# Register-addressed hardware loops for the products with wq and w3, and 15 small loads at the end, in a decode kernel on one core

## The chip, the cores and the metric

The kernel runs on one core of a Trainium2 chip. The metric is the device time of one execution in microseconds (us), the median of several runs. One execution was also taken by the hardware profiler; its instructions and transfers are what is called the trace here. The engines are TensorE (PE, whose weight loads have a row of their own, PEld), VectorE (DVE), ScalarE (ACT), GpSimd (POOL) and SyncE (SP). A name with a q behind it (PEldq, DVEq, SPq) stands for instructions that the engine's sequencer works off by itself: register arithmetic, branches, waits, and the issue of DMAs.

## What is computed

Two branches on the same two rows of x, mixed by a gate (`Sk` is 16384, `D` 1024, 32 heads of 128, `F` 3584; all inputs bf16):

```
g = sigmoid((x * gate_w).sum(-1))
q = x @ wq                                  # 1024 x 4096, in 32 heads
a = softmax(q k_cache^T * 128**-0.5) v_cache, heads joined, @ wo
h = gelu(layernorm(x) @ w1), shifted along the sequence
x1 = x + h @ w2                             # with one token the shift leaves zeros
b = x1 + gelu(layernorm(x1) @ w3) @ w4      # w3: 1024 x 3584, w4: 3584 x 1024
out = g * a + (1 - g) * b
```

There are 64 pairs of batch row and head. K and V of one pair are 4 MB (2^22 bytes) each, so the two caches make up 537 of the 570 million bytes that one execution reads.

## The kernel before

**The plan.** The program is written as a list of operations for each engine (`_Plan`). `pl.add` appends an instruction with the events that it waits for, and gives it an event of its own if it is to signal; an event is a semaphore and a count. `emit` writes the lists out. For TensorE, DVE and ACT the 32 rounds over the caches are written as a hardware loop of 16 turns with two rounds each (L100); inside it each wait compares with a count held in a register (L72), and one DVE instruction (L703) writes to an address held in a register. All that stands ahead of the rounds is written out in full, instruction by instruction.

**The ring.** All weights and caches pass through a ring in SBUF of five slots of 32 KB in each partition (4 MB a slot). SP issues every load of it, in one fixed order: wq (slots 0, 1), w2 (slot 2), w3 (3, 4), w4 (0, 1), then K and V of round 0, K and V of round 1 and so on, and the two halves of wo last, the second in six pieces. K of a round takes slots 2 and 3 or 3 and 4 by turns, V takes 0 and 1. A load is issued when the readers of its slots have released them (`release`, `pump`). So w4 waits for the last product with wq, K of round 0 waits for the reader of slot 3, and V of round 0 waits for the last product with w4.

**The prologue on TensorE.** x is transposed (L589). The product with wq (L604) has 8 steps over the rows of wq and 32 heads in each, 256 products of a 128x128 weight block with two columns, all into one PSUM bank; the first one of all clears the bank (`start`). DVE copies q out (L609). The products with w2 (L510) and the layer norm of x1 (L401 to L444) follow. The product with w3 (`dense_stage`, L468 to L490, matmul at L477) is put on the list eight times, once for each of the eight groups of rows of w3, with 28 output blocks each, 224 products. Slot 3 holds the first 16384 of a partition's 28672 elements, so it is released after the fifth group and slot 4 after the eighth. GELU (L454 to L462) and the product with w4 (L510) end the prologue; the row b goes to PSUM (L526, L529).

**The rounds.** DVE transposes K in place (L647), TensorE makes the scores (L653), DVE, ACT and TensorE the softmax, TensorE the product with V (L689), and L703 stores the pair's row.

**The end.** The heads are joined, the product with wo (L728) is added to the row in PSUM, DVE copies out each half (L757), and SP and ACT store a quarter each of either half (L760). All engines then meet (L789), SP waits for the last two stores, and its increment of a semaphore (L792) ends the program.

Of the kernel before, what the change touches and what calls it, by code (L numbers as in the profile page):

```python
# [9 lines left out]
BF16 = mybir.dt.bfloat16  # L10
# [13 lines left out]
class _Plan:  # L24
# [18 lines left out]
    def add(self, eng, fn, waits=(), sig=False, dyn=False):  # L43

        ev = None
        if sig:
            self.cnt[eng] += 1
            ev = _Ev(self.esem[eng], self.cnt[eng])
        self.ops[eng].append((self._merge(waits), fn, ev, 1, dyn))
        return ev  # L50

    def dma(self, eng, fn, sem, waits=()):
        key = sem.num
# [55 lines left out]
def _cdiv(a, b):  # L109
    return (a + b - 1) // b  # L110
# [10 lines left out]
def build_kernel(nc, A_x, A_k, A_v, A_wq, A_wo, B_w1, B_w2, B_w3, B_w4, gate_w, out, dbg=None):  # L121
    dbg = dbg or {}
    B, Sq, D = A_x.shape
    _, H, Sk, Dh = A_k.shape
    F = B_w3.shape[1]
# [13 lines left out]
    NBD = D // P  # L139
    NBF = F // P  # L140
    NRS = 5
    SLOT = J * Dh
# [25 lines left out]
    with ExitStack() as st:  # L168
        inner = st.enter_context(ExitStack())
        block = inner.enter_context(nc.Block())  # L170
        sb = lambda name, shape, dt: st.enter_context(nc.sbuf_tensor(name, shape, dt))
# [14 lines left out]
        xT_bf = sb("xT_bf", [P, NBD, 2], BF16)  # L186
# [30 lines left out]
        xn_bf = sb("xn_bf", [P, NBD, 2], BF16)  # L217
# [9 lines left out]
        banks = [st.enter_context(nc.psum_tensor(f"ps{i}", [P, 512], F32)) for i in range(8)]  # L227
        sem = lambda n: st.enter_context(nc.semaphore(n))
# [8 lines left out]
        pl = _Plan(esems)  # L237
# [38 lines left out]
        for hp in range(HP):  # L276
# [7 lines left out]
                    waits=(ev_rowm,), sig=True)  # L284
# [4 lines left out]
                        waits=(e0,), sig=True)  # L289
# [16 lines left out]
        def pump():  # L306
            while dma_q and all(i in slot_free for i in dma_q[0][2]):
                key, fns, slots = dma_q.pop(0)
                waits = sum((slot_free.pop(i) for i in slots), ())
                slot_of[key] = slots[0]  # L310
                slots_of[key] = slots
                for k, fn in enumerate(fns):
                    dsem = s_ring[slots[0]] if len(fns) == 1 else s_tail[k]
                    dma_done[key] = dma_done[key, k] = pl.dma("sp", (lambda e, fn=fn, idx=slots[0]: fn(e, idx)), dsem,
                                                              waits=waits if k == 0 else ())

        def release(key, ev, slots=None):
            for idx in slots or slots_of[key]:
                assert idx not in slot_free
                slot_free[idx] = tuple(ev) if isinstance(ev, (tuple, list)) else (ev,)  # L320
            pump()

        def arrived(key):
            assert key in dma_done, f"load {key} not yet issued in program order (would deadlock)"
            return dma_done[key]
# [50 lines left out]
        hs_ps, h3_ps = r3(hs_ps2d), r3(h3_ps2d)  # L376
        bc_nb = lambda ap2: ap2.unsqueeze(1).broadcast_to([P, NBD, 2])
        b5_rd = []
        evd = {}
# [3 lines left out]
        def pe_b5(fn, waits=(), sig=False):  # L383
            ev = pl.add("pe", fn, waits=tuple(waits) + tuple(b5_rd) + (evd["b5zero"],), sig=sig)
            del b5_rd[:]
            if sig:
                b5_lw[0] = ev
            return ev

        def b5_wrote(ev):  # L390
            b5_lw[0] = ev
# [73 lines left out]
        def cols(wv, kl, nb, nout):  # L465
            return wv[:, kl, :].rearrange("p (q r) -> p r q", r=nout)[:, nb, :]

        def dense_stage(key, kls, nkw, nout, out_ps, rhs_of, rhs_key, done_key, width):  # L468
            def run():
                wv = ring_w(slot_of[key], nkw, width)  # L470
                ev_arr = arrived(key)
                ev = None
                first = True
                for nb in range(nout):
                    for kl in kls:
                        lastmm = (nb == nout - 1 and kl == kls[-1])
                        fn = lambda e, nb=nb, kl=kl: e.matmul(  # L477
                            out_ps[:, nb, :], lhsT=cols(wv, kl, nb, nout), rhs=rhs_of(kl),
                            start=False, stop=True, skip_group_check=True)
                        if first:  # L480
                            ev = pe_b5(fn, waits=(ev_arr, evd[rhs_key]), sig=lastmm)
                            first = False
                        else:
                            ev = pl.add("pe", fn, sig=lastmm)
                for j, slot in enumerate(slots_of[key]):
                    if kls[-1] == _cdiv(min(nkw * width, SLOT * (j + 1)), width) - 1:
                        release(key, ev, (slot,))
                b5_wrote(ev)
                evd[done_key] = ev
            return run  # L490

        def st_x1():
# [44 lines left out]
        def put(fns, key=None):  # L537
            if key is not None:
                w_order.append(key)
            pro_stages.extend(fns)  # L540
# [16 lines left out]
        key = ("w2", 0)  # L557
        put([row_stage(key, list(range(NBD)), 0, NBD, lambda kc: shT_bf[:, kc, :], "const", last=True), hs_columns], key)
        put([st_x1, ln_a(x1T_f[:, :, :], "x1", st2_ps, "xn2"), ln_b(st2_ps, "xn2", None)])
        key = ("w3", 0)  # L560
        put([dense_stage(key, [kl], NBD, NBF, h3_ps, lambda kc: xn_bf[:, kc, :], "xn2", "h3", F) for kl in range(NBD)], key)
        put([gelu2])
        key = ("w4", 0)
        put([row_stage(key, list(range(k, k + kn)), 0, NBF, lambda kc: GT_bf[:, kc, :], "GT", last=(k + kn == NBF))
# [14 lines left out]
        for pi in range(2):  # L579
            queue_load(("wo", pi), wloads[("wo", pi)], ((2, 3)[pi],))  # L580
        pump()

        def xcols(row, b_n, nb):
            return row[0:b_n, :].rearrange("b (q r) -> b r q", r=NBD)[:, nb, :]
# [8 lines left out]
        ev_xT_bf = pl.add("dve", lambda e: e.tensor_copy(xT_bf[:, :, :], trv[:, :, 0:2]), waits=(ev_xtr,), sig=True)  # L593
        evd["xT_f"] = pl.add("dve", lambda e: e.tensor_copy(xT_f[:, :, :], trv[:, :, 0:2]), waits=(ev_xtr,), sig=True)
        evd["b5zero"] = pl.add("dve", lambda e: e.memset(B5[:, :], 0.0), sig=True)
        pl.add("dve", lambda e: e.memset(rows2_ps[:, :], 0.0), sig=True)
        ev_r0 = pl.add("dve", lambda e: e.memset(rows_ps[:, :], 0.0), sig=True)

        q_ps = banks[1][:, 0:H * 2].rearrange("p (h b) -> p h b", b=2)
        key = ("wq", 0)  # L600
        wv = ring_w(slot_of[key], NBD, HD)
        for kc in range(NBD):
            for h in range(H):
                ev = pl.add("pe", lambda e, h=h, kc=kc: e.matmul(  # L604
                    q_ps[:, h, :], lhsT=wv[:, kc, h * Dh:(h + 1) * Dh], rhs=xT_bf[:, kc, :], start=(kc == 0 and h == 0),
                    stop=(kc == NBD - 1), skip_group_check=True),
                    waits=(arrived(key), ev_xT_bf) if h == 0 else (), sig=(h == H - 1))
        release(key, ev)
        ev_q = pl.add("dve", lambda e: e.tensor_copy(q_sb[:, :, :], q_ps), waits=(ev,), sig=True)  # L609
        q4_ps = banks[2][:, 0:NBP * G].rearrange("p (t g) -> p t g", t=NBP)  # L610
# [96 lines left out]
        def do_aproj():  # L707
            or_ps = bank_bf(7)[0:G, 256:256 + P]
            o4_ps = banks[3][:, 0:B * RO].rearrange("p (b r) -> p b r", b=B)
            e1 = pl.add("pe", lambda e: e.transpose(or_ps, OT_sb[:, :], ident[:, :]), waits=(ev_OT,), sig=True)  # L710
            e2 = pl.add("dve", lambda e: e.tensor_copy(OR_sb[:, :], or_ps), waits=(e1,), sig=True)
            ev = None
            for b in range(B):
                for dq in range(QO):
                    ev = pl.add("pe", lambda e, b=b, dq=dq: e.matmul(
                        o4_ps[:, b, :], lhsT=esel[:, b, dq, :], rhs=OR_sb[:, RO * dq:RO * (dq + 1)], start=(dq == 0), stop=(dq == QO - 1),
                        skip_group_check=True), waits=(e2, ev_const) if b + dq == 0 else (), sig=(b == B - 1 and dq == QO - 1))
            ev_half = [None, None]
            ev_o4 = pl.add("dve", lambda e: e.tensor_copy(OT4_sb[:, :, :].rearrange("p r b -> p b r"), o4_ps), waits=(ev,), sig=True)
            for hi in range(2):  # L720
                key = ("wo", hi)
                wt = ring[:, slot_of[key], :].rearrange("p (r n) -> p r n", r=RS)
                for k, (r0, rn, q0, qn) in enumerate(wo_runs[hi]):
                    w = (dma_done[key, k], ev_o4, evd["bg"])
                    for r in range(r0, r0 + rn):
                        for qd in range(q0, q0 + qn):
                            ps = half(qd)
                            ev = pl.add("pe", lambda e, r=r, qd=qd, wt=wt, ps=ps: e.matmul(  # L728
                                ps[32 * qd:32 * qd + 2, 0:DQ], lhsT=OT4_sb[:, r, :], rhs=wt[:, r % RS, qd * DQ:(qd + 1) * DQ],
                                start=False, stop=True, tile_position=(0, 32 * qd), skip_group_check=True), waits=w,  # L730
                                sig=(qd == q0 + qn - 1))
                            w = ()
                            ev_half[qd // HQ] = ev
            return ev_half
# [14 lines left out]
        pl.mark[NPR] = {e: len(pl.ops[e]) for e in ENGS}  # L749
        assert not dma_q, "unissued DMAs remain"  # L750

        ev_alast = do_aproj()
        ev_out2 = []
        PH2 = P // 2
# [34 lines left out]
        inner.close()  # L789
        for ev in ev_out2:  # L790
            nc.sync.wait_ge(ev.sem, ev.val)
        nc.sync.sem_inc(s_end, 1)  # L792


# [45 lines left out]
```

## Time and profile before

| | us |
|---|---|
| median of 3 runs | 1324.66 (1324.58 to 1324.75) |
| the profiled execution | 1324.56 |
| its span, first to last instruction | 1323.0 |
| TensorE products busy | 785.5 |
| TensorE weight loads busy | 335.6 |
| DVE busy | 660.0 |
| ACT busy | 45.7 |

TensorE had 0.791 of its full clock on average. The span begins with the first instruction and ends with the last; the 1.5 us beside it are the start and end of the execution, which hold no instruction of the kernel. Rows of the timeline give the start, the length, engine, line, operation, what is written and read, how many instructions are merged, and in brackets the idle time in front and what ended it. Rows of one line give a count, the shortest, median and longest instruction in ns, and the starts of the first and the last.

### The profile page before, as it was taken

What the parts mean: (1) busy time and instruction counts of PE and PEld (TensorE: products, weight loads), DVE (VectorE), ACT (ScalarE), POOL (GpSimd) and SP (SyncE); (2) the same over time, 40 slices, a digit from 0 to 9 for tenths busy, and PEclk for the clock granted to TensorE, in tenths of its full rate; (3) what the DMA queues carried; (4) which work ended last, traced back from release to release, by engine and by line L of the source; (5) the groups of instructions that cost most, each with busy time, mean ns of one, the idle gap of its engine ahead of it and who ended that gap; (6) DMA issues with size and microseconds to landing.
All of it is one profiled execution on the core that took longest, in us unless ns stands there. A gap on an engine that the chain in (4) does not pass through costs nothing.

```text
span 1323.0 us, 12293 instructions
## 1 busy us (share of the span) xinstructions
PE 785.5 (59%) x5235; PEld 335.6 (25%) x5235; DVE 660.0 (50%) x527; ACT 45.7 (3%) x99; POOL 23.6 (2%) x110
## 2 busy tenths in 40 slices
PE   2645567656556765655676565567565556756457
PEld 2512222222222222222222222222222222222223
DVE  0254446655444665544466554446655445665444
ACT  0000000000000000000000000000000000000000
POOL 3000000000000000000000000000000000000000
PEclk9977778776777877677787767888877778887778
DMA  9999999999999999999999999999999999999998
GB/s 413 437 430 433 430 434 436 430 436 434 430 438 434 430 438 432 430 438 432 430 438 432 430 438 432 430 438 432 430 438 432 434 436 430 434 436 430 436 434 367
DMA packets 10976, 570.59 MB, mean 431 GB/s; under 512 B 1219, under 2 KB 1747, under 8 KB 1878
## 3 DMA queue, kind: packets, MB, share of 16 engines
q1 hardware_dynamic: 10936, 570.43, 99.7%
q8 instruction: 8, 0.13, 0.0%
q10 hardware_dynamic: 30, 0.01, 0.0%
q14 instruction: 2, 0.02, 0.0%
HBM read 570.44 MB, written 0.00 MB: 431 GB/s over the span
## 4 chain that ended last, share of the span: by engine, by line
DMA 70%; PE 23%; DVE 6%; issue 0%; SPq 0%
DMA ring<-in_A_k_cache_dram 65%; PE ps L653 23%; DVE ring L647 6%; DMA ring<-in_B_w_dram 3%; DMA ring<-in_A_wo_dram 2%; PE ps L477 1%; SPq L331 0%; PE ps L728 0%; DVE orow L757 0%
## 5 line engine op out<-in xcount | busy, mean ns | idle before, releaser
L653 PE MATMUL ps<-ring,Z 128*128 128x512 bf16 x2048 | 533.4, 419 | 388.4 <-DVE ring L647 387.6
L647 DVE STREAM_TRANSPOSE ring<-ring 128x2048 f32<-128x2048 f32 x256 | 565.2, 2275 | 276.2 <-DMA ring<-in_A_k_cache_dram 276.2
L653 PEld LDWEIGHTS ps<-ring,Z 128*128 128x128 bf16 x2048 | 203.4, 104 | 705.7 <-issue 469.3
L689 PE MATMUL ps<-ring,PT_sb 128*32 128x512 bf16 x2048 | 169.9, 505 | 3.9 <-DVE recip L680 3.5
L703 DVE SCALAR_TENSOR_TENSOR OT_sb<-ps,gT,recip 128x2 f32 x32 | 7.0, 219 | 204.9 <-PE ps L700 204.9
L689 PEld LDWEIGHTS ps<-ring,PT_sb 128*32 128x32 bf16 x2048 | 67.9, 123 | 92.0 <-issue 71.3
L674 ACT ACTIVATE P_sb<-ps,negm 128x512 bf16<-128x512 f32 x32 | 22.0, 687 | 1006.3 <-DVE negm L672 1006.3
L663 DVE TENSOR_REDUCE rA<-ps 128x1 f32<-128x512 f32 x32 | 22.1, 692 | 64.2 <-PE ps L653 64.2
L678 PE MATMUL ps<-rowsum,hsel 128*128 128x1 f32 x128 | 24.3, 293 | 38.0 <-ACT P_sb L674 38.0
L676 DVE STREAM_TRANSPOSE PT_sb<-P_sb 128x512 bf16<-128x512 bf16 x32 | 22.8, 712 | 27.0 <-ACT P_sb L674 27.0
L634 POOL TENSOR_TENSOR Z<-q_f,mask 128x8 bf16<-128x8 f32 x64 | 12.3, 228 | 1207.7 <-PE ps L653 1207.7
L678 PEld LDWEIGHTS ps<-rowsum,hsel 128*128 128x128 f32 x128 | 21.5, 239 | 40.7 <-ACT P_sb L674 40.7
L665 PE MATMUL ps<-ident,rmax_bf 128*1 128x128 bf16 x32 | 6.9, 217 | 33.1 <-DVE rmax_bf L664 33.1
L698 ACT ACTIVATE acc_sb<-ps 128x512 bf16<-128x512 f32 x32 | 19.1, 597 | 200.6 <-PE ps L689 200.6
L700 PE MATMUL ps<-dsel,acc_sb 128*128 128x2 bf16 x128 | 8.1, 167 | 22.5 <-ACT acc_sb L698 22.5
L477 PE MATMUL ps<-xn_bf,ring 128*128 128x2 bf16 x224 | 14.4, 202 | 3.6 <-DMA ring<-in_B_w_dram 3.6
L604 PE MATMUL ps<-xT_bf,ring 128*128 128x2 bf16 x256 | 7.1, 165 | 14.6 <-DMA ring<-in_A_wq_dram 11.9
L477 PEld LDWEIGHTS ps<-xn_bf,ring 128*128 128x128 bf16 x224 | 14.3, 162 | 3.6 <-DMA ring<-in_B_w_dram 3.6
L700 PEld LDWEIGHTS ps<-dsel,acc_sb 128*128 128x128 bf16 x128 | 5.3, 96 | 38.3 <-ACT acc_sb L698 38.3
L665 PEld LDWEIGHTS ps<-ident,rmax_bf 128*1 128x1 bf16 x32 | 2.5, 79 | 48.9 <-DVE rmax_bf L664 48.9
L666 DVE TENSOR_REDUCE m_sb<-ps 1x2 bf16<-1x128 bf16 x32 | 8.9, 279 | 9.9 <-PE ps L665 9.9
L672 DVE TENSOR_SCALAR negm<-ps,cAB 128x1 f32<-128x1 f32 x32 | 8.9, 278 | 9.2 <-PE ps L669 9.2
(98 smaller groups left out, 88.7 us busy)
## 6 DMA issues: line engine op xcount, KB each, us to landing
ring<-in_B_w_dram SPq DMA_DIRECT2D x2, 7168.0 KB, 37.1
ring<-in_A_wo_dram SPq DMA_DIRECT2D x1, 4096.0 KB, 38.6
ring<-in_B_w_dram SPq DMA_DIRECT2D x1, 2048.0 KB, 26.5
ring<-in_A_wo_dram SPq DMA_DIRECT2D x1, 2048.0 KB, 22.8
ring<-in_A_wo_dram SPq DMA_DIRECT2D x1, 1024.0 KB, 25.0
ring<-in_A_k_cache_dram SPq DMA_DIRECT2D x32, 26.9
ring<-in_A_v_cache_dram SPq DMA_DIRECT2D x32, 29.2
ring<-in_A_wo_dram SPq DMA_DIRECT2D x1, 512.0 KB, 25.8
```

What stands on the lines that cost most here:

```text
L477: fn = lambda e, nb=nb, kl=kl: e.matmul(out_ps[:, nb, :], lhsT=cols(wv, kl, nb, nout), rhs=rhs_of(kl), start=False, stop=True, skip_group_ ...
L634: ev = pl.add("pool", lambda e, hp=hp: e.tensor_tensor(Z[:, :, ZO:ZO + P].rearrange("p t (i c) -> p t i c", c=32)[:, :, 2 * hp:2 * hp + 2, ...
L647: return pl.add("dve", lambda e: e.transpose(ap, ap), waits=(arrived(("k", n)),), sig=True)
L653: ev = pl.add("pe", lambda e, bp=bp: e.matmul(S_ps[:, 0:NCOL], lhsT=Z[:, bp, ZO - 2 * u:ZO - 2 * u + P], rhs=kv[:, :, bp // 2, :, bp % 2], ...
L663: e1 = pl.add("dve", lambda e: e.tensor_reduce(rA[:, :], S_ps[:, 0:NCOL], axis=AX.X, op=ALU.max), waits=(ev_S[n],), sig=True)
L665: e3 = pl.add("pe", lambda e: e.transpose(mt_ps, rmax_bf[:, :], ident[:, :]), waits=(e2,), sig=True)
L674: e7 = pl.add("act", lambda e: e.activation(P_sb[:, :], S_ps[:, 0:NCOL], ACT.Exp, bias=negm[:, 0:1], scale=scale, accum_out=rowsum[:, 0:1] ...
L676: e8 = pl.add("dve", lambda e: e.transpose(PT_sb[:, :], P_sb[:, :]), waits=(e7,), sig=True)
L678: e9 = pl.add("pe", lambda e, hp=hp: e.matmul(l_ps[:, hp:hp + 1], lhsT=hsel[:, hp, :], rhs=rowsum[:, 0:1], start=True, stop=True, skip_gro ...
L689: ev = pl.add("pe", lambda e, jj=jj, cg=cg: e.matmul(acc_ps[32 * cg:32 * cg + 32, 0:512], lhsT=PT_sb[:, 32 * jj:32 * jj + 32], rhs=vv[:, 4 ...
L698: e1 = pl.add("act", lambda e: e.activation(acc_sb[:, :], acc_ps[:, 0:512], ACT.Copy), waits=(ev_pv,), sig=True)
L700: e2 = pl.add("pe", lambda e, w=w: e.matmul(oT_ps, lhsT=acc_sb[:, w * P:(w + 1) * P], rhs=dsel[:, w, :], start=(w == 0), stop=(w == 3)), w ...
```

## The change

A new method, `turns`, puts a hardware loop on an engine's list. It takes a list of functions that each write one instruction with the turn's number, and the number of turns; the last instruction of a turn signals, so there is one event for each turn. The waits stand ahead of the loop.

The products with wq become such a loop of eight turns with 32 products, the products with w3 one of eight turns with 28. Weight block and column pair are addressed with the turn's number, which is in a register of TensorE. The order of the products and the turns at which slots are released stay. q's PSUM columns are now zeroed by DVE beforehand, and no product clears the bank.

Behind the last load of wo, SP gets 15 more loads, of 2 to 16 rows of 64 bytes from w2 into a tile that nothing reads, each with a semaphore of its own. At the very end SP waits for all 15, behind its waits for the stores.

```diff
+    def turns(self, eng, fns, count, waits=()):
+        base, sem = self.cnt[eng], self.esem[eng]
+        self.cnt[eng] += count
+
+        def run(e):
+            with e.Fori(0, count) as i:
+                for fn in fns:
+                    ins = fn(e, i)
+                ins.then_inc(sem, 1)
+        self.ops[eng].append((self._merge(waits), run, None, 1, False))
+        return [_Ev(sem, base + n + 1) for n in range(count)]
...
-        def dense_stage(key, kls, nkw, nout, out_ps, rhs_of, rhs_key, done_key, width):
+        def dense_stage(key, nkw, nout, out_ps, rhs, rhs_key, done_key, width):
...
-                for nb in range(nout):
-                    for kl in kls:
-                        lastmm = (nb == nout - 1 and kl == kls[-1])
-                        fn = lambda e, nb=nb, kl=kl: e.matmul(
-                            out_ps[:, nb, :], lhsT=cols(wv, kl, nb, nout), rhs=rhs_of(kl),
-                            start=False, stop=True, skip_group_check=True)
...
+                waits = (arrived(key), evd[rhs_key], evd["b5zero"]) + tuple(b5_rd)
+                del b5_rd[:]
+                evs = pl.turns("pe", [lambda e, i, nb=nb: e.matmul(
+                    out_ps[:, nb, :], lhsT=wv[:, bass.ds(i, 1), :].rearrange("p o (q r) -> p (o r) q", r=nout)[:, nb, :],
+                    rhs=rhs[:, bass.ds(i, 1), :].rearrange("p o b -> p (o b)"),
+                    start=False, stop=True, skip_group_check=True) for nb in range(nout)], nkw, waits)
                 for j, slot in enumerate(slots_of[key]):
-                    if kls[-1] == _cdiv(min(nkw * width, SLOT * (j + 1)), width) - 1:
-                        release(key, ev, (slot,))
+                    release(key, evs[_cdiv(min(nkw * width, SLOT * (j + 1)), width) - 1], (slot,))
...
+        ptile = sb("ptile", [16, 16, 32], BF16)
+        s_probe = [sem(f"pb{i}") for i in range(16)]
...
+        ev_q0 = pl.add("dve", lambda e: e.memset(banks[1][:, 0:H * 2], 0.0), sig=True)
...
-        for kc in range(NBD):
-            for h in range(H):
-                ev = pl.add("pe", lambda e, h=h, kc=kc: e.matmul(
-                    q_ps[:, h, :], lhsT=wv[:, kc, h * Dh:(h + 1) * Dh], rhs=xT_bf[:, kc, :], start=(kc == 0 and h == 0),
-                    stop=(kc == NBD - 1), skip_group_check=True),
-                    waits=(arrived(key), ev_xT_bf) if h == 0 else (), sig=(h == H - 1))
+        ev = pl.turns("pe", [lambda e, i, h=h: e.matmul(
+            q_ps[:, h, :], lhsT=wv[:, bass.ds(i, 1), h * Dh:(h + 1) * Dh].rearrange("p o d -> p (o d)"),
+            rhs=xT_bf[:, bass.ds(i, 1), :].rearrange("p o b -> p (o b)"),
+            start=False, stop=True, skip_group_check=True) for h in range(H)], NBD, (arrived(key), ev_xT_bf, ev_q0))[-1]
...
+        for k in range(2, 17):
+            pl.dma("sp", lambda e, k=k: e.dma_start(ptile[0:k, k - 1, :], B_w2[0:k, 0:32]), s_probe[k - 1])
         ev_alast = do_aproj()
...
         for ev in ev_out2:
             nc.sync.wait_ge(ev.sem, ev.val)
+        for k in range(2, 17):
+            nc.sync.wait_ge(s_probe[k - 1], 16)
         nc.sync.sem_inc(s_end, 1)
```

More of the change, by code (lines that the diff above doesn't have):

```diff
@@ L466, in cols @@
             return wv[:, kl, :].rearrange("p (q r) -> p r q", r=nout)[:, nb, :]
-        def dense_stage(key, kls, nkw, nout, out_ps, rhs_of, rhs_key, done_key, width):
+        def dense_stage(key, nkw, nout, out_ps, rhs, rhs_key, done_key, width):
             def run():
                 wv = ring_w(slot_of[key], nkw, width)
-                ev_arr = arrived(key)
-                ev = None
-                first = True
-                for nb in range(nout):
-                    for kl in kls:
-                        lastmm = (nb == nout - 1 and kl == kls[-1])
-                        fn = lambda e, nb=nb, kl=kl: e.matmul(
-                            out_ps[:, nb, :], lhsT=cols(wv, kl, nb, nout), rhs=rhs_of(kl),
-                            start=False, stop=True, skip_group_check=True)
[L480 to L484, printed above, removed]
+                waits = (arrived(key), evd[rhs_key], evd["b5zero"]) + tuple(b5_rd)
[4 more added lines that the diff above has]
+                    start=False, stop=True, skip_group_check=True) for nb in range(nout)], nkw, waits)
                 for j, slot in enumerate(slots_of[key]):
-                    if kls[-1] == _cdiv(min(nkw * width, SLOT * (j + 1)), width) - 1:
-                        release(key, ev, (slot,))
-                b5_wrote(ev)
-                evd[done_key] = ev
+                    release(key, evs[_cdiv(min(nkw * width, SLOT * (j + 1)), width) - 1], (slot,))
+                b5_wrote(evs[-1])
+                evd[done_key] = evs[-1]
             return run
@@ L560, in build_kernel @@
         key = ("w3", 0)
-        put([dense_stage(key, [kl], NBD, NBF, h3_ps, lambda kc: xn_bf[:, kc, :], "xn2", "h3", F) for kl in range(NBD)], key)
+        put([dense_stage(key, NBD, NBF, h3_ps, xn_bf, "xn2", "h3", F)], key)
         put([gelu2])
```

## The prediction, made before the result

> **What bounds the kernel now.** I read the page's shares and its chain first, then the chain in order of time, then the timeline of the first 70 us, then the waits of SP.
>
> ```profile
> span 1323.0 us, 12293 instructions
> DMA  9999999999999999999999999999999999999998
> q1 hardware_dynamic: 10936, 570.43, 99.7%
> DMA 70%; PE 23%; DVE 6%; issue 0%; SPq 0%
> 1.67 44.16 DMA ring<-in_B_w_dram
> 54.95 27.18 DMA ring<-in_A_k_cache_dram
> ```
>
> SP's queue alone keeps the 16 DMA engines busy for 99.7% of the span, in every slice. So a hole in that queue's transfers is paid in full, since nothing later runs below capacity and could make it up; what is hidden behind the transfers is free. The question is whether the slowed products make SP issue a load too late.
>
> ```profile
> 0.74 0.41 SPq L331 DMA_DIRECT2D ring<-in_A_wq_dram  x1
> 1.20 31.90 SPq L331 DMA_DIRECT2D ring<-in_B_w_dram  x3
> 17.57 0.48 DVE L597 MEMSET ps<- 128x512 f32 x1
> 22.89 5.87 PE L604 MATMUL ps<-xT_bf,ring 128*128 128x2 bf16 x214 [11.92 <-DMA ring<-in_A_wq_dram]
> 31.48 1.26 PE L604 MATMUL ps<-xT_bf,ring 128*128 128x2 bf16 x42 [2.72 <-issue]
> 32.78 0.23 DVE L609 CAST q_sb<-ps 128x64 bf16<-128x64 f32 x1 [14.73 <-PE ps L604]
> 43.36 0.18 DVE L444 TENSOR_TENSOR xn_bf<-zc,mv 128x16 bf16<-128x16 f32 x1 [0.83 <-POOL mv L442]
> 45.88 14.36 PE L477 MATMUL ps<-xn_bf,ring 128*128 128x2 bf16 x224 [3.55 <-DMA ring<-in_B_w_dram]
> 54.95 0.33 SPq L361 DMA_DIRECT2D ring<-in_A_k_cache_dram  x1
> 61.99 0.22 DVE L462 TENSOR_TENSOR GT_bf<-gl_b,gl_x 128x56 bf16<-128x56 f32 x1
> 62.83 4.49 PE L510 MATMUL ps<-ring,GT_bf 128*2 128x256 bf16 x112 [2.59 <-DMA ring<-in_B_w_dram]
> 67.37 0.33 SPq L365 DMA_DIRECT2D ring<-in_A_v_cache_dram  x1
> ring<-in_A_wq_dram SPq DMA_DIRECT2D x1, 22.1
> SPq L331 <- PE ps L604: 30.6, 1, 30.6
> SPq L361 <- PE ps L477: 21.8, 1, 21.8
> ```
>
> Two issues hang on the products that change. w4's load waits for the last wq product (30.6 us of waiting); the first K load waits for w3's product rows 0 to 4, that is 140 of 224 products (21.8 us). Today both are early: w4 is issued at about 32.8, while w3 is still landing (45.88), and K at 54.95, while w4 is still landing (62.83). The row of wq (8 MB into an idle queue) gives 22.1 us from issue to landing, and K is as large; it landed at 54.95 + 27.18 = 82.13 because it stood behind w4. It could have been issued 27.18 - 22.1 = 5.1 us later at no cost. Ahead of that, w3's products waited from 43.54 (43.36 + 0.18) to 45.88 for their weights, 2.3 us. So the two product stages may grow by 7.4 us together before the queue runs dry.
>
> **The change part by part.** *The register addresses.* The trace holds no TensorE product with a register address, so its price is bounded by the sequencer's rows. The main loop shows what TensorE's sequencer takes for register work, and L703 is the one compute instruction with a register address, on DVE:
>
> ```profile
> L72 PEldq ALU_OP  x416: 32/32/42, 84.6 to 1309.3; - x139
> L72 DVEq ALU_OP  x208: 40/40/52, 102.6 to 1313.0; - x104
> L100 PEldq FUSED_REGOPS  x16: 50/50/50, 66.6 to 1232.7; - x16
> L100 DVEq FUSED_REGOPS  x16: 62/63/63, 69.3 to 1233.2; - x16
> L100 PEldq ALU_OP  x16: 32/32/32, 150.1 to 1312.7; - x16
> L100 PEldq COMPARE_BRANCH  x16: 83/215/243, 150.2 to 1312.8; - x16
> L703 DVEq FUSED_REGOPS  x32: 71/73/81, 112.0 to 1313.1; - x32
> 1312.69 0.25 PE L700 MATMUL ps<-dsel,acc_sb 128*128 128x2 bf16 x4 [0.71 <-ACT acc_sb L698]
> 1313.19 0.22 DVE L703 SCALAR_TENSOR_TENSOR OT_sb<-ps,gT,recip 128x2 f32 x1 [7.44 <-PE ps L700]
> 1313.46 0.24 PE L710 MATMUL ps<-ident,OT_sb 128*64 128x128 bf16 x1 [0.52 <-DVE OT_sb L703]
> 1313.75 0.22 DVE L711 COPY OR_sb<-ps 64x128 bf16<-64x128 bf16 x1 [0.34 <-PE ps L710]
> ```
>
> The copy at L711 starts 0.05 us after the product that it waits for (1313.46 + 0.24 to 1313.75). L703 starts 0.25 us after its own (1312.94 to 1313.19). The 0.20 us between them are two register instructions on DVE's sequencer, one for the wait (40 ns) and one for the address (73 ns), so 0.20 - 0.113 = 0.087 is gaps, 44 ns for each. TensorE's sequencer takes 50 where DVE's takes 63, a factor 0.8: a gap of 35 ns, and an address of 0.8 x 73 = 58 ns. Each turn uses another weight address for each of its 32 (wq) or 28 (w3) products, so I count one register instruction for each product: from 32 + 35 = 67 ns (a plain ALU_OP) to 58 + 35 = 93 ns. The product itself then goes through as today: 5.87 us / 214 = 27 ns at L604. That makes c = 94 to 120 ns for a product; I take 110, nearer to L703, because that row is an address and the ALU_OP rows are waits. The 14.36 / 224 = 64 ns that w3's products take today lies below it, so c holds there too.
>
> *The turns.* The end of a turn has an ALU_OP, a branch and a FUSED_REGOPS at L100: 32 + 215 + 50, and three gaps of 35, t = 0.40 us. The sequencer is what limits these stages, so t isn't hidden. The Trainium skill ("Advanced Engine Details and Errata", Control Flow Timing) gives a compare-and-branch about 108 ns, where this trace has a median of 215; with 108 the sum below would be 13 x 0.107 = 1.4 us less. The measured row is used.
>
> *The sum.* Products of wq: 256 x 0.110 + 8 x 0.40 = 31.4 us from 22.89, so they end at 54.3 (today 32.74, of which 2.72 us was a stall that the shorter program loses). w4's load is issued there, about 8.5 us after w3 has landed: the first hole. From the last wq product to xn_bf today's chain takes 43.54 - 32.74 = 10.8 us, of which nothing changes; it is ready at 65.05. Five turns of w3 take 140 x 0.110 + 5 x 0.40 = 17.4: K is issued at 82.45, by when w4 has long landed, and lands 22.1 later at 104.55, against 82.13. In general the loss is 396c + 13t - 26.3 us (396 products and 13 turns stand before that issue); with c = 0.110 it is **22.4 us**, in two holes of the DMA.
>
> What is late next: V's load waits for w4's products. After K's issue come 84c + 3t = 10.4 us of w3, then 2.1 of GELU (60.24, where L477 ends, to 62.3, just after L462), and 4.5 of w4's products, together 17.0. V's transfer may follow K's if V is issued by 22.1 - 2.8 = 19.3 after K (2.8 is 22.1 less the 19.3 us from w4's landing to K's landing, that is the start of a lone load). It fits by 2.3; should the 2.72 us stall move into this part, 0.4 us is lost. Everything from there on repeats as today.
>
> *The zeroing of q's bank* is a DVE memset of an eighth of L597's width (0.48 us); DVE then idles for 14.73 us before L609, five of them before wq lands. Free; uncovered it would be under 0.5 us.
>
> *The 15 small loads.*
>
> ```profile
> 1272.02 0.33 SPq L365 DMA_DIRECT2D ring<-in_A_v_cache_dram  x1
> 1272.39 21.89 SPq L331 DMA_DIRECT2D ring<-in_A_wo_dram  x4
> 1294.33 1.41 SPq L337 DMA_DIRECT2D ring<-in_A_wo_dram  x3
> SPq L760 <- DVE orow L757: 25.6, 2, 25.4
> 1320.96 0.27 PE L728 MATMUL ps<-ring,OT_sb 128*2 128x256 bf16 x2
> 1321.17 0.82 SPq L760 DMA_DIRECT2D out_dram<-orow  x2
> L789 SPq EVENT_SEMAPHORE  x1: 17/17/17, 1322.7 to 1322.7; - x1
> L792 SPq EVENT_SEMAPHORE  x1: 189/189/189, 1322.8 to 1322.8; - x1
> ```
>
> Three loads are issued in 1.41 us, so 15 take 15 x 0.47 = 7.1 us, in the 25.4 us that SP then waits for the output row. They stand behind the last weights in the queue, so these aren't delayed, and hold 8.5 KB in all (135 rows of 64 bytes). The output stores, behind them on SP, are issued 0.9 us after the last piece of wo is there (1320.3). Bounds on this: 0 to 1 us; I take 0, as 8.5 KB is nothing beside the pieces in front of it. The 15 waits on SP stand behind the last barrier, where L792 ends the span, and are paid: 15 x 17 ns = 0.3 us if only busy time counts, 15 x 0.189 = 2.8 as L792 goes; with 17 + 35 ns each, **0.8 us**, which is nearer to L789 since all are long satisfied.
>
> The profiled execution took 1324.56 us (span 1323.0), 0.10 below the median of 1324.66. So 1324.66 + 22.4 + 0.8 = **1347.9 us**.
>
> **The rivals.** *The sequencer also handles each register-addressed weight load and product itself.* Then both cost a step of 32 + 35 = 67 ns like an ALU_OP, 134 in place of 27, and c = 217. Loss at K: 396 x 0.217 + 5.2 - 26.3 = 64.8; V then comes late too: 19.4 + 2.1 + 4.5 + 2.8 - 22.1 = 6.7. Time 1324.66 + 71.5 + 0.8 = 1397 us. For it: the 27 ns today can't hold such a step. Against: L703's own delay is used up by its two register instructions. The Trainium skill ("TensorE: Matmul & The Clock Gate", Wait — 56ns, not 53.3ns?) states this step as about 62 ns for a product that the hardware does not decode by itself, and says nothing of register addresses; with 62 the time would be about 1392.
>
> *The other side: no register instruction per product.* If the constant part of the address rides in the instruction and one register serves a turn, c stays at 27 and 64 ns, the loops cost their turns alone (8 x 0.40 = 3.2 for wq, less than the 2.72 stall that goes plus the slack of 7.4), no load is late, and 0.8 us at the end remains: 1325.5. It decides as long as c is below about 53 ns. For it: the main loop's waits need one ALU_OP where two operations are meant, so common parts are kept. Against: L703 pays a full FUSED_REGOPS at both of its places, in the same turn, with addresses that differ by a constant.
>
> *The queue holds SP.* If SP can't put 23 loads in flight, the 15 go out after wo has landed, 7.1 us from 1320.3 on, and the output is 1327.4 - 1321.17 = 6.2 us late. Against: one, four and three loads since 1272.02 were under way at 1295.8, when SP had come to its wait at L760, so eight don't hold it. It adds to any case.
>
> **How the numbers follow.** The forecast (one register step per product, c from 75 to 150) 0.52; the handled products 0.23; no register instruction 0.17; something between, such as two register steps per product at c = 0.17 (46 us), 0.08; held SP 0.05 within these. Forecast's own range, c 94 to 120: 1341 to 1355 (with both ends of the waits on SP). As the no-change case alone holds 0.17 and the dear one 0.23, neither can be left out: 1325 to 1397. Two tenths of a per cent, 2.6 us, is about what can be told from no change here. Faster would need transfers that run faster or start earlier, and no part touches that: 0.02. Within: 0.17. Slower: 0.81.
>
> **What would show it.** Right: a row of ALU_OP or FUSED_REGOPS on PEldq, some 480 of them, at the line of the loops; products of wq lasting about 31 us and of w3 28; DMA digits below 9 in slices 2 and 3 of 40; the first K load issued near 82; 32 equal rounds after it; L792 followed by more semaphore rows. Wrong: products at 27 ns and full DMA slices (no change), or products over 150 ns with a third hole before V (the dear case), or a loss that lies behind 1300 us of the span.

## The result, and the profile after

| | before | after |
|---|---|---|
| median of 4 runs, us | 1324.68 (1324.58 to 1324.75) | 1356.97 (1356.37 to 1358.02) |
| the profiled execution, us | 1324.56 | 1358.02 |
| its span, us | 1323.0 | 1356.7 |

The kernel became slower by 32.3 us, a ratio of 1.0245 (95% interval 1.0233 to 1.0257). The forecast was 1347.9, in a range of 1325 to 1397. The profiled execution of after is 1.05 us above its median.

The page of after, its header, the transfers in 40 slices of 33.9 us, SP's queue, and the shares of the chain that ended last:

```profile
span 1356.7 us, 12847 instructions
DMA  9459999999999999999999999999999999999998
GB/s 418 202 247 429 430 431 433 431 433 433 433 433 439 433 435 433 433 433 433 433 435 433 433 433 433 435 433 433 433 433 433 433 433 435 435 437 435 437 433 359
q1 hardware_dynamic: 11206, 570.44, 97.4%
DMA 67%; PE 26%; DVE 6%; issue 1%; SPq 0%; POOL 0%
```

The queue carries the same 570.4 MB, and its share falls from 99.7%. The second and third slices hold the whole fall: 202 and 247 GB/s, every later slice is as full as before. Nothing makes the holes up. The chain in order of time says whose they are (start, length, what):

```profile
0.74 22.21 DMA ring<-in_A_wq_dram
23.32 4.16 PE ps L609 x32
...
87.27 3.67 PE ps L486 x28
90.96 23.09 DMA ring<-in_A_k_cache_dram
```

Before, the chain went from the load of w3 (44.16 us) through five groups of w3's products to K:

```profile
45.88 9.05 PE ps L477 x140
```

Now it goes through the products with wq, the layer norm and five turns of w3 before K can be issued. The timeline has their times:

```profile
1.21 58.72 SPq L344 DMA_DIRECT2D ring<-in_B_w_dram  x3
23.32 4.16 PE L609 MATMUL ps<-xT_bf,ring 128*128 x32 [12.38 <-DMA ring<-in_A_wq_dram]
...
55.42 4.15 PE L609 MATMUL ps<-xT_bf,ring 128*128 x32 [0.43 <-issue]
...
70.19 0.18 DVE L457 TENSOR_TENSOR xn_bf<-zc,mv 128x16 bf16<-128x16 f32 x1 [0.84 <-POOL mv L455]
70.84 3.79 PE L486 MATMUL ps<-xn_bf,ring 128*128 x28 [1.69 <-DVE xn_bf L457]
...
87.27 3.66 PE L486 MATMUL ps<-xn_bf,ring 128*128 x28 [0.40 <-issue]
90.96 0.33 SPq L374 DMA_DIRECT2D ring<-in_A_k_cache_dram  x1
...
105.28 5.73 PE L514 MATMUL ps<-ring,GT_bf 128*2 128x256 bf16 x112 [2.11 <-DVE GT_bf L475]
111.05 0.33 SPq L378 DMA_DIRECT2D ring<-in_A_v_cache_dram  x1
```

The first row merges the issues of w2, w3 and w4: the third, w4, is issued at 59.60, just before the row's end, when the last wq product is done. A turn now is a row of its own with a gap behind it. wq's products run from 23.32 to 59.57 (36.25 us; before, 5.87 + 1.26 and a stall of 2.72); xn_bf is ready at 70.37 (before 43.54); K is issued at 90.96 (before 54.95) and lands at 114.05 (before 82.13), **31.9 us later**. The waits of SP tell the same from the other side (us in total, times, longest):

```profile
SPq L344 <- PE ps L609: 57.5, 1, 57.5
SPq L374 <- PE ps L486: 31.0, 1, 31.0
SPq L767 <- DVE orow L764: 6.6, 2, 6.4
```

Before, SP's waits for wq and w3 were 30.6 and 21.8 us. The windows of 40 to 60 and 80 to 100 us show the holes themselves (busy time of PE, PEld, DVE, ACT and POOL, granted clock, DMA share, GB/s):

```profile
40.00:60.00 20.00, 17.96 (x141) 14.41 (x142) 0.23 (x1) 0.00 (x0) 0.00 (x0) 1.00 0.11 49
80.00:100.00 20.00, 17.97 (x139) 17.43 (x139) 0.00 (x0) 0.00 (x0) 0.00 (x0) 1.00 0.45 184
```

TensorE looks busy at 90% while the DMA share is down to 0.11 and 0.45. Its granted clock is 1.00, so the clock is not what is missing. What takes the time stands in the rows of the loops' lines on TensorE's sequencer (shortest, median, longest in ns; first and last start):

```profile
L609 PE MATMUL ps<-xT_bf,ring x256: 163/183/185, 23.3 to 59.4; 128*128 x128
L609 PEldq FUSED_REGOPS  x248: 46/46/46, 23.4 to 59.3; - x124
L609 PEldq ALU_OP  x8: 36/36/42, 23.2 to 55.3; - x8
```

```profile
L486 PEldq FUSED_REGOPS  x224: 42/46/51, 70.7 to 102.8; - x112
```

```profile
L58 PEldq FUSED_REGOPS  x16: 78/78/87, 23.1 to 99.3; - x16
L58 PEldq COMPARE_BRANCH  x16: 76/208/225, 27.4 to 103.1; - x16
```

There is one register instruction for each product: 248 FUSED_REGOPS and 8 ALU_OP for wq's 256 products, 224 for w3's 224. From the rows of the timeline, a product takes (4.15 - 0.183)/31 = 0.128 us where it took 0.027; the last product of a turn and the first of the next start 0.183 + 0.43 = 0.61 us apart, so a turn costs 0.61 - 0.128 = 0.48 us more. In the single records of the trace the usual cycle is 124 ns: the register instruction 46, then 49 until the weight load starts, 7 until the product starts, and 22 until the next register instruction. About one cycle in nine takes some 150 ns, which makes the mean of 128. The cycle is the same for w3's products, which took 64 ns before.

SP's timeline at the end shows the small loads:

```profile
1329.86 18.54 SPq L758 DMA_DIRECT2D ptile<-in_B_w_dram  x15
1354.84 0.73 SPq L767 DMA_DIRECT2D out_dram<-orow  x2
```

The 15 issues take 18.5 us in front of the output stores, and SP then still waits 6.4.

From K on: V lands 20.2 us after K (111.05 + 23.2, against 114.05) where it was 19.35, so another 0.85 us is lost there, and the last waits of SP take 0.59 us instead of 0.34. 31.9 + 0.85 + 0.25 are 33.0 of the 33.7 us between the two spans; the rest is not assigned, and lies within what this one execution is above its median.

### The profile page after: what moved, and what is told of

It reads as the page before. It is cut to its first block, busy times and chain, and to the rows that moved or that the text cites. A ratio compares the mean times of both kernels' runs of the same rounds, so it can differ in the third digit from the quotient of the medians.

```text
span 1356.7 us, 12847 instructions
## 1 busy us (share of the span) xinstructions
PE 832.4 (61%) x5235; PEld 371.4 (27%) x5235; DVE 660.0 (49%) x528; ACT 45.7 (3%) x99; POOL 23.6 (2%) x110
## 4 chain that ended last, share of the span: by engine, by line
DMA 67%; PE 26%; DVE 6%; issue 1%; SPq 0%; POOL 0%
DMA ring<-in_A_k_cache_dram 63%; PE ps L658 22%; DVE ring L652 5%; PE ps L609 2%; DMA ring<-in_A_wo_dram 2%; DMA ring<-in_A_wq_dram 2%; PE ps L486 1%; DVE hsd L548 0%; PE ps L514 0%; PE ps L414 0%; SPq L344 0%; PE ps L733 0%; POOL mv L455 0%; DVE orow L764 0%; DVE q_f L621 0%
## 5 line engine op out<-in xcount | busy, mean ns | idle before, releaser
L694 PE MATMUL ps<-ring,PT_sb 128*32 128x512 bf16 x2048 | 174.3, 516 | 4.1 <-DVE recip L685 3.7
L668 DVE TENSOR_REDUCE rA<-ps 128x1 f32<-128x512 f32 x32 | 22.1, 691 | 64.2 <-PE ps L658 64.2
L609 PE MATMUL ps<-xT_bf,ring 128*128 x256 | 33.1, 183 | 15.5 <-DMA ring<-in_A_wq_dram 12.4
L609 PEld LDWEIGHTS ps<-xT_bf,ring 128*128 x256 | 26.6, 104 | 22.0 <-issue 15.9
L486 PE MATMUL ps<-xn_bf,ring 128*128 x224 | 29.5, 223 | 4.5 <-issue 2.9
L486 PEld LDWEIGHTS ps<-xn_bf,ring 128*128 x224 | 28.5, 143 | 5.5 <-issue 5.2
## 6 DMA issues: line engine op xcount, KB each, us to landing
ring<-in_A_wo_dram SPq DMA_DIRECT2D x1, 1024.0 KB, 24.4
```

What stands on the lines that cost most here:

```text
L486: evs = pl.turns("pe", [lambda e, i, nb=nb: e.matmul(out_ps[:, nb, :], lhsT=wv[:, bass.ds(i, 1), :].rearrange("p o (q r) -> p (o r) q", r= ...
L609: ev = pl.turns("pe", [lambda e, i, h=h: e.matmul(q_ps[:, h, :], lhsT=wv[:, bass.ds(i, 1), h * Dh:(h + 1) * Dh].rearrange("p o d -> p (o d)"),
L668: e1 = pl.add("dve", lambda e: e.tensor_reduce(rA[:, :], S_ps[:, 0:NCOL], axis=AX.X, op=ALU.max), waits=(ev_S[n],), sig=True)
L694: ev = pl.add("pe", lambda e, jj=jj, cg=cg: e.matmul(acc_ps[32 * cg:32 * cg + 32, 0:512], lhsT=PT_sb[:, 32 * jj:32 * jj + 32], rhs=vv[:, 4 ...
```

## The experiments

The theory after the result: one register instruction per product, which adds 97 ns to wq's 27, takes the place of the weight loads' own pace, TensorE's sequencer becomes the bound of both stages, and the holes are what is left after the slack. The rivals: a product with a register address is itself slow; the loop's turns and branches cost it; the small loads or the waits cost part of it.

**The loops without the 15 loads (e_loops: after, less two pieces).**

```diff
-        for k in range(2, 17):
-            pl.dma("sp", lambda e, k=k: e.dma_start(ptile[0:k, k - 1, :], B_w2[0:k, 0:32]), s_probe[k - 1])
...
-        for k in range(2, 17):
-            nc.sync.wait_ge(s_probe[k - 1], 16)
```

> Both loops, without the 15 small loads and their waits. Theory (a register step for each product holds back w4 and the first K load): all of the loss but the 0.25 us of the waits stays, 1356.7 us, the first K load issued near 91 us and landed near 114. Rival (the small loads cost a part, as SP was held in issuing them for 18.5 us): 1355 or less.

1357.12 us, 1.0248 (1.0233 to 1.0264): the whole loss. K is issued at 90.95, as in after. The loads are no measurable part of it.

**The 15 loads and their waits without the loops (e_loads: before, plus the same two pieces).**

> The kernel before with the 15 small loads and their waits alone. Theory: SP is held at the issues for some 18 us but has 25 us, so only the waits behind the last barrier are paid: 1324.9 to 1325.0. Rival (the loads delay wo's last pieces or the output): 1326 or more.

1324.63 us, 0.9999 (0.999 to 1.0008): no change. But SP was not free. Its timeline near the end:

```profile
1295.71 19.45 SPq L768 DMA_DIRECT2D ptile<-in_B_w_dram  x15
1321.29 0.84 SPq L777 DMA_DIRECT2D out_dram<-orow  x2
```

The issues take 19.5 us, not 7.1, and still end 6 us before the output row. The same issues in narrow windows, one by one, the first three and the last:

```profile
1295.71 4.59 SPq L768 DMA_DIRECT2D ptile<-in_B_w_dram  x1
1300.34 3.54 SPq L768 DMA_DIRECT2D ptile<-in_B_w_dram  x1
1304.31 2.00 SPq L768 DMA_DIRECT2D ptile<-in_B_w_dram  x1
...
1314.78 0.39 SPq L768 DMA_DIRECT2D ptile<-in_B_w_dram  x1
```

In front of the first small load are eight loads that have not landed, V and the seven pieces of wo. The issue of this ninth load takes 4.59 us, and the ones behind it less. The first hold ends at 1300.3, before the first of the eight, V, has landed as a whole (1301.4), so it is not simply the number of loads in flight that lets SP go on.

**The loop for wq alone (e_wq), and the loop for w3 alone (e_w3)**, without the loads: each is after with the other loop written out again as before (dense_stage or the products with wq).

```diff
-        put([dense_stage(key, NBD, NBF, h3_ps, xn_bf, "xn2", "h3", F)], key)
+        put([dense_stage(key, [kl], NBD, NBF, h3_ps, lambda kc: xn_bf[:, kc, :], "xn2", "h3", F) for kl in range(NBD)], key)
```

```diff
-        ev = pl.turns("pe", [lambda e, i, h=h: e.matmul(
...
+        for kc in range(NBD):
+            for h in range(H):
+                ev = pl.add("pe", lambda e, h=h, kc=kc: e.matmul(
...
```

> The loop for wq alone, w3 written out as before. Theory (only what passes the slack of the loads is lost): products end at 59.6, xn ready at 70.4, K issued after 140 x 65 ns at 79.5 and landed 23.1 later at 102.6, 20.4 later than before: 1345. Rival (the products' added time counts in full, 256 x 0.0975 us and the turns, 26.7 us): 1351.

> The loop for w3 alone, wq written out as before. Theory: w3 starts at 46.3, K is issued 20.1 later at 66.4 and lands 23.1 later at 89.5, 7.4 late, and V's load then comes about 1 us late as well: 1333. Rival (added time in full, 224 x 0.06 us and the turns, 18 us): 1343.

wq alone: 1345.43 us, 1.0157 (1.0141 to 1.0172). w3 alone: 1332.85 us, 1.0061 (1.0046 to 1.0076). SP's first issue of K in wq alone, then in w3 alone:

```profile
79.36 0.33 SPq L374 DMA_DIRECT2D ring<-in_A_k_cache_dram  x1
```

```profile
66.67 0.33 SPq L374 DMA_DIRECT2D ring<-in_A_k_cache_dram  x1
```

The two losses, 20.6 and 8.1 us, make 28.7, less than the 32.3 of both loops (1357.12 - 1324.80). The first K tells why: it lands at 102.73, 88.57 and, with both loops, 114.13, that is 20.6, 6.4 and 32.0 us later than before. The issues of K do add up: they come 24.4 and 11.7 us late alone, and 36.0 with both. The landings are each some 4 to 5 us less late than the issues. The difference, 32.0 - 27.0 = 5.0, is the 5.1 us by which K could be late at no cost: alone, each loop has them, together they have them once. Behind the first K, w3 alone loses another 1.4 us until K of round 1 lands (7.8 late there): V, issued 19.2 us after K, lands 1.1 later behind K than before, and K of round 1 adds 0.2. With wq's loop alone nothing is lost there, with both loops 0.3, in after 1.2; what sets the size is open. The parts of a change do not add where they draw on one slack.

**Both loops, all addresses constant (e_static).** Each turn multiplies the same row group.

```diff
-            q_ps[:, h, :], lhsT=wv[:, bass.ds(i, 1), h * Dh:(h + 1) * Dh].rearrange("p o d -> p (o d)"),
-            rhs=xT_bf[:, bass.ds(i, 1), :].rearrange("p o b -> p (o b)"),
+            q_ps[:, h, :], lhsT=wv[:, 0, h * Dh:(h + 1) * Dh],
+            rhs=xT_bf[:, 0, :],
```

and the same in dense_stage, with row group nkw - 1.

> Both loops of eight turns with constant addresses and no small loads; each turn multiplies the same group of rows (the first of wq, the last of w3), so seven eighths of the two products are left out and one is added eight times. Theory (the register step is the price): products 27 and 64 ns apart, the turns under 0.7 us each, no load late: 1324.7 to 1325. Rival (the loop itself keeps TensorE's sequencer from running ahead): products still near 120 ns apart, 1350 or more.

1324.68 us, 1.0 (0.9991 to 1.0009). TensorE's timeline:

```profile
23.03 6.96 PE L609 MATMUL ps<-xT_bf,ring 128*128 128x2 bf16 x256 [12.01 <-DMA ring<-in_A_wq_dram]
...
44.86 14.33 PE L486 MATMUL ps<-xn_bf,ring 128*128 128x2 bf16 x224 [5.29 <-DMA ring<-in_B_w_dram]
```

27 and 64 ns per product, eight turns merged into one row with no gap between them. So the loops and their branches cost nothing here: the first turn's branch starts at 23.53, 0.35 us before the second turn's first product (23.88). The 0.48 us of a turn shows only in the kernels where the sequencer is the bound.

**The right side by register, the weights constant (e_rhsreg).**

```diff
-            q_ps[:, h, :], lhsT=wv[:, bass.ds(i, 1), h * Dh:(h + 1) * Dh].rearrange("p o d -> p (o d)"),
+            q_ps[:, h, :], lhsT=wv[:, 0, h * Dh:(h + 1) * Dh],
             rhs=xT_bf[:, bass.ds(i, 1), :].rearrange("p o b -> p (o b)"),
```

> Both loops, the two columns of the right side addressed by register, the weights by constants (one group of rows is used eight times, the others are left out), no small loads. Theory (a register instruction is what costs, and one serves a turn): products near 27 and 64 ns apart, 1325. Rival (the sequencer handles a register-addressed product itself): some 50 to 70 ns more for each product, wq 20 to 25 us long, 1325 to 1337.

1324.72 us, 1.0 (0.999 to 1.001):

```profile
23.10 7.27 PE L609 MATMUL ps<-xT_bf,ring 128*128 x256 [12.33 <-DMA ring<-in_A_wq_dram]
```

28 ns per product. The right side has one address in a turn, and at this line there is no register instruction at all; the loop's own line has one FUSED_REGOPS for each turn.

**Both sides by register, but one weight block for all products of a turn (e_oneaddr).**

```diff
-            q_ps[:, h, :], lhsT=wv[:, bass.ds(i, 1), h * Dh:(h + 1) * Dh].rearrange("p o d -> p (o d)"),
+            q_ps[:, h, :], lhsT=wv[:, bass.ds(i, 1), 0:Dh].rearrange("p o d -> p (o d)"),
```

and `r=nout)[:, 0, :]` in dense_stage.

> Both loops with weights and right side by register, but one weight block for all products of a turn (the other blocks are left out), so no register instruction between products; no small loads. Theory: near 27 and 64 ns apart, 1325. Rival (handled by the sequencer): what is left of 124.5 ns without the 46 of the register instruction, 78 ns; wq 24 us, w3's five turns 13.7, less the 7.4 of slack: 1336 to 1337.

1324.81 us, 1.0 (0.9991 to 1.001). The timeline, then the rows of wq's line:

```profile
23.37 7.97 PE L609 MATMUL ps<-xT_bf,ring 128*128 x256 [12.50 <-DMA ring<-in_A_wq_dram]
...
45.19 14.35 PE L486 MATMUL ps<-xn_bf,ring 128*128 x224 [4.26 <-DMA ring<-in_B_w_dram]
```

```profile
L609 PEldq ALU_OP  x8: 36/36/42, 23.3 to 30.2; - x8
```

This is the run that decides. Weight loads and products are all addressed by a register, and run at 31 and 64 ns. Two things differ from after: there are 8 register instructions for wq's 256 products in place of 256, and the 32 products of a turn use the same weight block. That another block for each product costs nothing by itself shows in e_static, where the blocks change and the products run at 27 ns. So the price is the instruction between the products, and not the addressing. The Trainium skill ("TensorE: Matmul & The Clock Gate", Wait — 56ns, not 53.3ns?) gives a step of about 62 ns to a product that the hardware does not decode by itself; products with a register address do not fall under it here.

**A register loop where there is slack (e_tail: before, with row groups 5 to 7 of w3 as a loop of three turns).**

```diff
-        put([dense_stage(key, [kl], NBD, NBF, h3_ps, lambda kc: xn_bf[:, kc, :], "xn2", "h3", F) for kl in range(NBD)], key)
+        put([dense_stage(key, [kl], NBD, NBF, h3_ps, lambda kc: xn_bf[:, kc, :], "xn2", "h3", F) for kl in range(5)]
+            + [dense_tail(key, 5, NBD, NBF, h3_ps, xn_bf, "xn2", "h3", F)], key)
```

dense_tail is the new dense_stage with `bass.ds(i + k0, 1)`, k0 being 5, and one release at its end.

> Only the last three groups of rows of w3 as a register-addressed loop of three turns, all else as before, no small loads. Theory: K's load does not wait for them; w3 ends 7 us later, the products with w4 then end near 75, and V's load has until 78: no loss, 1324.4 to 1325. Rival (added time counts in full): 1331 to 1332.

1324.68 us, 1.0 (0.9991 to 1.0009). The last two turns, and the first V:

```profile
58.48 3.79 PE L510 MATMUL ps<-xn_bf,ring 128*128 x28 [0.44 <-issue]
62.69 3.76 PE L510 MATMUL ps<-xn_bf,ring 128*128 x28 [0.41 <-issue]
```

```profile
73.11 0.33 SPq L378 DMA_DIRECT2D ring<-in_A_v_cache_dram  x1
```

These turns are as slow as in after, and V is issued 5.7 us later than before (67.37). It costs nothing: K, issued in time, lands at 82.3 (before 82.1), and V is issued 18.0 us after K. The same slow products are paid in one place and free in the other; what decides is whether a load hangs on them that the queue needs next.

**The 15 loads with 16 rows each (e_loads16, a single run).**

```diff
+            pl.dma("sp", lambda e, k=k: e.dma_start(ptile[0:16, k - 1, :], B_w2[0:16, 0:32]), s_probe[k - 1])
```

> The kernel before with 15 small loads of 16 rows each. If SP is held because the DMA engines' queues are full of earlier descriptors, the first issues again take 3.5, 3.5 and 2 us and all 15 some 18 us, whatever the rows. If it is the few rows that make an issue slow (2 rows took 3.6 us, 16 rows 0.39), all 15 take 0.39 us each, 6 to 7 us in all.

1325.66 us in a single run, where before had 1324.71: 0.95 more, which one run cannot tell from chance. The issues took 20.2 us in place of 19.5, so the rows of the small loads do not make the hold. The rows show at the end, where the waits of SP now name the loads themselves (0.8 us in five waits). They land one by one, 0.2 us apart, the last at 1324.2 (issued at 1316.5), 0.1 us before the end of the span. In the run with 2 to 16 rows the last one landed at 1322.9, and SP's waits did not have to wait for any.

**45 loads (e_loads45).**

```diff
+        for m in range(3):
+            for k in range(2, 17):
+                ev_pb[k] = pl.dma("sp", lambda e, k=k, m=m: e.dma_start(ptile[0:k, 16 * m + k - 1, :], B_w2[0:k, 0:32]), s_probe[k - 1])
...
+            nc.sync.wait_ge(s_probe[k - 1], 48)
```

> The kernel before with 45 small loads (2 to 16 rows, three times) and 15 waits. Theory (held SP, cover of 25.4 us): 15 take 18.5 us, 30 more at 0.35 to 0.5 us another 10 to 15, so SP comes to the output 4 to 8 us late: 1329 to 1334. Rival (the hold of 18 us has nothing to do with the number of loads, or 45 x 0.47 = 21 us fit in): 1325.

1329.98 us, 1.004 (1.0025 to 1.0054):

```profile
1295.83 31.21 SPq L770 DMA_DIRECT2D ptile<-in_B_w_dram  x45
1327.09 0.57 SPq L779 DMA_DIRECT2D out_dram<-orow  x2
```

The first 15 issues take 19.3 us, the other 30 take 11.9. SP comes to the output stores at 1327.09, 5.8 us later than with 15 loads, and the kernel is 5.3 us slower. So the cover is finite: 15 loads use some 19 of 25 us, 45 use it up.

## Why the prediction was right, and where its sizes were off

**The bound and the place: right.** A queue that is full in every slice, two issues that hang on the products, two holes before the first K, and full slices from there on: all as forecast. e_loops, e_wq, e_w3 and e_tail show that the slow products cost what they delay in the loads. The slack of 7.4 us came out as 6.0 in e_wq (wq's products end 26.65 us later there, and K lands 20.6 later), and as 7.3 when its longer landing is added (23.4 in place of 22.1).

**The range: met because it was wide.** It reached from 1325 to 1397 to take in the two rivals. The forecast's own range for one register step per product was 1341 to 1355 (its upper terms, 26.4 and 2.8 us, make 1354), and the measured 1356.97 lies above it, as c = 0.128 lies above the bounds of 0.094 to 0.120.

**The step that was mis-sized: the register instruction.** The prediction took 58 ns and one gap of 35, so at most c = 0.120 with the product's own 27, and chose 0.110. It measured 46 ns busy and 51 of gaps, 97 together, 124 with the product's 27 in the usual cycle and 0.128 in the mean. The instruction was sized too long and the gap, scaled from DVE's by 0.8, too short: DVE's gap, scaled, did not give TensorE's. 396 x 0.018 is **7.1 us**, most of what the forecast lacks.

**The rest of the 9.5 us at K's landing** (114.05 against 104.55): a turn at 0.48 instead of 0.40, on the eleven edges inside the two loops, comes to about 0.1 us more than the 13 whole turns that were counted; the starts of the two loops, from their data to their first product, add 0.4 and 0.47, which were not counted (23.32 against 22.89, of which 0.1 is a later landing of wq, and 70.84 against 70.37); the landing took 23.1 in place of 22.1. The landing was 23.2 in the kernel with the loops alone, 23.4 with wq's loop (where w4 was still landing for 0.7 us of it), and 21.9 with w3's, so a K load into an idle queue is not always dearer than wq's (22.21 in the same execution as K's 23.09); why it was here is not known. 7.1 + 0.1 + 0.9 + 1.0 = 9.1; the 0.4 left is rounding and the tail of the last product.

**V: forecast to fit by 2.3 us, it lost 0.85.** V was issued 20.1 us after K (111.05 - 90.96) where the prediction had 17.0. The 84 products and three turns took 12.2 instead of 10.4, GELU 2.1 as forecast, and w4's products 5.73 instead of 4.49. The prediction's limit of 19.3 us does not say how much is lost: with the loops alone V was issued 20.0 us after K and lost 0.1, with w3's loop alone it was issued after 19.2 and lost 1.1. The prediction had allowed that the stall of 2.72 us in wq's products, which is gone, might turn up here, and these 1.2 us stand in that place. But e_loads speaks against a stall that merely moved: it has both, 2.90 us in wq's products and 5.96 us for w4's. What lengthens w4's products is open.

**The turn's branch.** 208 ns is the median of the compare-and-branch here, where the prediction took 215 from the trace of before. The Trainium skill ("Advanced Engine Details and Errata", Control Flow Timing) gives about 108, so taking the measured row was right.

**The small loads: free, but not as argued.** The price of 15 x 0.47 us was too low by a factor of 2.6: SP was held for 18.5 us in after. From "eight loads don't hold SP" nothing followed for the ninth. The conclusion held by luck: the wait of 25.4 us was long enough to hide that too, and 6.4 of it were left. The waits cost 0.25 us in the trace and nothing that the time shows, below the 0.3 that was the low end. They were not "long satisfied" either: the last small load landed at 1356.44, 0.25 us before the end of the span.

**The rivals.** "No register instruction per product" failed by its own condition: c is 0.128 and not below 0.053. Its price was right, though: e_oneaddr, where one address serves a turn, took 1324.81 us, and the rival's 1325.5 is 1324.7 without the waits, which e_oneaddr lacks. "The sequencer handles each product itself" is refuted by e_oneaddr and e_rhsreg. "The queue holds SP" happened in part, but inside the cover; e_loads45 shows it decide. The zeroing of q's bank did not show: DVE was done with it before wq had landed.

## What to carry to other kernels

In a hardware loop, count the different addresses in a turn, not the operands with a register: with one weight address for a turn the time did not change, while an address for each small product made every product 128 ns long, where wq's had taken 27 and w3's 64. Ask of a slower stage which load hangs on its end, and how early that load was issued: such loops cost 32 us in front of issues that the queue needed next, and three turns behind K's issue cost nothing in e_tail, where V still came in time. Work on an idle issuing engine is free only up to its wait, and that wait is to be compared with the time for which the queue holds the engine, not only with the time of an issue into a queue with room.

## What the runs showed of the hardware

- SP is held when it issues behind many loads that have not landed: behind eight, of 128 KB to 8 MB, the ninth took 3.6 to 5.4 us to issue in four runs, the next two 3.5 to 3.6 and 2.0, and later ones mostly 1.2 to 0.3, as against 0.3 to 0.5 for the eight. The rows of the small loads (2 to 16, or 16 each) made no difference to that. What exactly is full does not show in the trace.
- A register instruction of 46 ns on TensorE's sequencer between every two products made the usual step from product to product 124 ns, 97 more than wq's and 60 more than w3's step without it.
- Eight turns of 32 or 28 products at constant addresses ran without a visible gap, although each turn has a branch of some 210 ns: in e_static the first branch began 0.35 us before the product behind it.
